# Attention of one batch moved to array quarters and ahead of the last weight loads, in a fused retention and expert kernel

## The chip, the cores and the metric

The kernel runs on one core of one Trainium2 chip. The metric is the device time of one execution in microseconds (us). The kernel before took 515.71 us, the median of 6 runs (515.15 to 519.15).

## What is computed

The reference has two parts, and the output of the first is the input of the second. Cut to what matters:

```python
# q, k, v: 8 batches x 8 heads x 576 positions x 64
scores = (q @ k.T) / 8                       # for each batch and head
Dmat   = gamma[h] ** (i - j) where i >= j, else 0
x      = ((scores * Dmat) @ v), heads side by side   # 4608 tokens x 512

# 4 experts, w1: 512 x 1024, w2: 1024 x 512
p   = probs / (probs.sum(-1) + 1e-9)
out = sum over e of p[:, e] * (relu(x @ w1[e]) @ w2[e])   # 4608 x 512
```

The first part is a retention layer: attention with a decay instead of a softmax. The second sends every token through all four experts, and adds their outputs with weights.

## The kernel before

**Work and order.** The 4608 tokens are cut into nine tiles of 512. A *unit* (nt, e) is tile nt in expert e: an *up* part that makes the hidden values `relu(x @ w1[e])`, and a *down* part that multiplies them with `w2[e]`. There are 36 units, and the order of every instruction is written out by hand: nothing is rescheduled, so each engine works through its own queue in the order in which the Python code issues to it.

**Two ways of working a unit.** The classical way (`up_classical` L522, `downs` L544) takes 32 products of 128 x 128 weights with 512 columns for each part; their lines in the profile are L525 (tile `ph`) and L564 (tile `po`). The other way (`up_fast` L678, class `Down` L625) splits both matrices into 2 x 2 blocks and forms the block product with seven block products instead of eight, 56 products of 256 columns for each part; the lines are L691 (tiles `upP`, `upQ`, `upR`, by PSUM bank) and L645 (`downV`, `downW`). It needs sums of blocks, made by VectorE (DVE): of the weights (`weight_sums` L580, `down_sums` L603), once for each expert; of the tokens (`token_sums` L597), once for each tile; and of the hidden values (`hidden_sum` L608), for each unit. In `up_fast`, DVE reads bank P twice for each half: once into `upR` (L707), once into the hidden values (L715), which GpSimd (POOL) then clamps at zero (L716). TensorE writes that bank again afterwards.

**Attention.** Each batch's 576 positions are four chunks of 128 and a remainder of 64. Three classes work it. `AttP` (L406) is for batch 0: its loads take positions in pairs, its scores and values are products on quarters of the array, 64 rows by 64 columns, and a visit handles four heads by 256 positions. `Att` (L251) is for the others: a visit handles a chunk of 128 positions for all heads, with products on halves of the array. A visit is made of transposes (T), scores (S), the chunk's key-value product (kv), and the output (O), to which the states of the earlier chunks are added through `sbd`. `put_x` (L232) copies the output into the token tiles. The batches from 2 on go through a planner (`Chain`, L779): a list for each engine from which the unit loop takes the next piece at set places, at most when what it needs has been issued.

**The front.** POOL issues the weight loads, which also convert to 16 bits, in its own software DMA queue; SyncE (SP) issues the loads of q, k and v and the plain stores in the hardware queue. Batch 0 is loaded first, then the weights of all four experts one behind the other (L736 to L759), all of them issued by 24 us. SP then loads batch 0's remainder, whose first load waits for the first `w2` (`load_next(w20)`), and after it batch 1 chunk by chunk (`load_piece` L109). On TensorE the front is a list of classical work, `head` (L731, L986): up (0,0), up (0,1), down (0,0), down (0,1), up (0,2), down (0,2), up (0,3), down (0,3), up (1,0). It is cut into groups, counted by `g`, and the dictionary `plan`, filled by `at(g, ...)` (L914 to L984), says what is issued behind which group: batch 0's remainder at 29 to 34, batch 1's four chunks at 39 to 47, and the weight sums in between.

**The loop behind it** (L1019) begins with unit (1,1). Each turn issues `up_fast` of its unit, and between its products the down part of the unit before (`fill`), the planner's pieces and the sums still owed (`pay`). Down (1,0) is the last classical part.

**Outputs.** Tile 0 and the last tile are summed over the experts on the chip (`on_chip` L500) and stored at the end. For the others, expert 0's part is stored by SP, and the others are added in memory by POOL's accumulating stores (L514).

Of the kernel before, what the change touches and what calls it, by code (L numbers as in the profile page):

```python
# [23 lines left out]
def kernel(  # L24
# [66 lines left out]

    def raw_units(b):

        state[b] = {}
        for x in range(4):
            t = wpool.tile([128, 3, H * D], FP32, tag=f"w2s_{x}", name="raw")
            for i, (n, _) in enumerate(SRC):
                state[b][n, x] = t[:, i]

    def load_paired(b):  # L100
        raw_units(b)
        for x, (hf, u) in enumerate(UNITS):
            h = slice(4 * u, 4 * u + 4)
            for n, src in SRC:
                nc.sync.dma_start(
                    out=state[b][n, x].rearrange("p (h x) -> p h x", h=4),
                    in_=src[b, h, 256 * hf:256 * hf + 256, :].rearrange("h (p j) d -> p h (j d)", j=2))
# [48 lines left out]
    load_paired(0)  # L156
# [249 lines left out]
    class AttP(Att):  # L406

        rem_states = (1, 3)

        def cast(self, n, hf, u, eng):  # L410
            if (n, u) == ("k", 0):
                self.half(hf)
            h = slice(4 * u, 4 * u + 4)
            if n != "v":
                self.m[n, hf, u] = att1.tile([128, 2, 4, D], BF16, tag=n + "m", name=n + "m", bufs=3)
            o = self.m[n, hf][:, :, h, :] if n == "v" else self.m[n, hf, u]
            i = self.t[n, 2 * hf + u].rearrange("p (h j d) -> p j h d", h=4, j=2)
            if n in gain:
                g = gain[n][:, NCH + 1 + 2 * hf:NCH + 3 + 2 * hf, h]
                eng.tensor_tensor(o, i, g.unsqueeze(3).to_broadcast([128, 2, 4, D]), op=MULT)  # L420
            else:
                eng.tensor_copy(o, i)
# [71 lines left out]


# [4 lines left out]
    def on_chip(nt):  # L500
        return nt in (0, n_nt - 1)

    def out_pair(nt, e, pair, j):

        if e == 0 or not on_chip(nt):
            acc[nt, j] = apool.tile([128, 2, Dm], FP32, tag="acc", name="acc")
        return acc[nt, j]

    def send(nt, e, pair, j):
        x = slice(nt * NSUB + pair[0], nt * NSUB + pair[1] + 1, pair[1] - pair[0])  # L510
        if e == 0:
# [32 lines left out]
    def downs(nt, e, ring):  # L544

        hT = hTs[nt, e]
        def evacuate(po, ns):
# [3 lines left out]
            if e == 0 or not on_chip(nt):  # L551
                nc.scalar.activation(a, po, Copy, scale=pe)
            else:
                nc.vector.scalar_tensor_tensor(a, po, pe, a, op0=MULT, op1=ADD)
            if not on_chip(nt):
                if ns % 2:
                    send(nt, e, pair, j)
            elif e == E - 1:
                nc.sync.dma_start(out=out[t * 128:(t + 1) * 128, :], in_=a)
# [65 lines left out]
    class Down:  # L625
# [37 lines left out]
        def out(self, i):  # L663
# [5 lines left out]
            if e and on_chip(nt):  # L669
# [5 lines left out]
            if i == 1 and not on_chip(nt):  # L675
                send(nt, e, pair, j)
# [80 lines left out]
    for e in range(2, E):  # L757
        load_w1(e)
        load_w2(e)  # L759
# [4 lines left out]
    for c in range(2):  # L764
        for n in "kqv":
            load_piece(1, n, c)
# [12 lines left out]
    class Chain:  # L779
        def __init__(self):  # L780
# [5 lines left out]
            self.now, self.begun, self.tokens, self.late = 0, {(1, "r"): -1}, 2 * S - R, []  # L786
# [87 lines left out]
        def emit(self, kind, nt, strict=True):  # L874
# [4 lines left out]
            for k, n in need.items():  # L879
# [8 lines left out]
                elif k == "tile":  # L888
                    ok = n <= nt + 2
# [27 lines left out]
    def casts1(*cs):  # L917
        for c in cs:
            for n in "kqv":
                state["a1"].cast(n, c, nc.gpsimd)  # L920

    def begin1():
        state["a1"] = Att(1)
        casts1(0)
        for c in range(2, NCH):
            for n in "kqv":
                load_piece(1, n, c)
        casts1(1, 2)
        load_ahead(7)

# [4 lines left out]

    def rem1_casts():
        for n in "kqv":
            a1().cast_rem(n, nc.gpsimd)
            loads["cast"] += 1
            load_ahead(len(PIECES))  # L940
        a1().dmaT(NCH)

    def a1():
        return state["a1"]
# [3 lines left out]
    at(29, a0.Trem)  # L948
    at(31, a0.Srem, a0.Srem_mask)
    at(34, a0.Orem, lambda: a0.x(NCH, nc.vector))  # L950
    at(25, begin1)
    for c, g in enumerate((39, 41, 43, 45)):
        at(g, lambda c=c: a1().T(c))
        at(g + 1, lambda c=c: (a1().S(c), a1().kv_chain(c)))
        if c > 0:
            at(g + 1, lambda c=c: a1().O(c - 1))
        at(g + 1, lambda c=c: (a1().mask(c, 0), a1().mask(c, 1)))
        if c > 0:
            at(g + 1, lambda c=c: a1().x(c - 1, nc.vector))
    at(47, lambda: (a1().O(3), a1().x(3, nc.vector)))  # L960

    def narrow():
        RINGS["at"] = ("a0", "a1", "a2")
        turn.update(at=0)

    at(42, lambda: casts1(3))
    at(46, rem1_casts)
    at(48, narrow, lambda: state.update(t1=token_sums(1)), lambda: [state["t1"].pop(i)() for i in (0, 0, 1)])

    def sums_at(kind, e, *gs):  # L970
        todo = []
        for i, g in enumerate(gs):
            at(g, lambda i=i: (todo or todo.extend(kind(e)), todo[i]()))
        return todo

    sums_at(weight_sums, 1, 16, 17, 18, 19)
    s0 = sums_at(weight_sums, 0, 20, 21, 22)
    sums_at(weight_sums, 2, 26, 28, 30, 31)
    sums_at(down_sums, 1, 42, 43, 44, 48)
    sums_at(weight_sums, 3, 36, 38, 49, 50)  # L980
    s2 = sums_at(down_sums, 2, 51, 52, 53)
    at(50, lambda: a1().put_krem(nc.gpsimd, a1().qr[:, 1]))
    for g in range(48, 56):
        at(g, lambda: pool(1, 1))  # L984

    head += [up_classical(0, 1), down_groups(0, 0), down_groups(0, 1), up_classical(0, 2), down_groups(0, 2),  # L986
             up_classical(0, 3), down_groups(0, 3), up_classical(1, 0, lead=2, cut=3 * NT // 4)]
    g = 0
    for work in head:
        for _ in work:  # L990
# [3 lines left out]
            if g > 48:  # L994
                chain.now += 1


    turn.update(po=0)
    state["t1"].pop()()
    def stage(nt, e):  # L1000
        return nt * E + e

    begin = {1: (1, 1), 2: (1, 2), 3: (1, 3), 0: (2, 0)}
    owed = [((1, 1), (2, 0), s0[3]), ((1, 1), (1, 3), s2[3])]
    for e in (3, 0):

        use, last = stage(*begin[e]) + 1, stage(*begin[e]) - E + 2
        owed += [(divmod(last if i == 3 else 0, E), divmod(use, E), f) for i, f in enumerate(down_sums(e))]

    def pay(nt, e, late=False):  # L1010
        for x in owed:
            if x[1] <= (nt, e) if late else x[0] <= (nt, e):
# [5 lines left out]
    before, gaps = (1, 0), 0  # L1018
    for nt, e in [(nt, e) for nt in range(1, n_nt) for e in range(E)][1:]:  # L1019
        fast = before >= begin[before[1]]  # L1020
# [8 lines left out]
        def between(i):  # L1029
# [3 lines left out]
            if i == 3:  # L1033
                pool(nt, 4 if gaps < 8 else 3 - g)
# [4 lines left out]
        def fill(i):  # L1039
            if i == 4:  # L1040
                chain.put_late()
            if not fast:
# [29 lines left out]
        def last_sum():  # L1072
            if g == 1 and (nt, e) >= begin[e]:
# [5 lines left out]
        def sums(i):  # L1079


            old, new = before in hsum, (nt, e) >= begin[e]
            turns = {(0, 1): 0 if old else 2, (0, 2): 0 if old else 1, (0, 3): 1,
                     (1, 1): 2, (1, 2): 1, (1, 3): 1}[g, i]
            while (e, g, i) == (0, 0, 2) and front:
# [4 lines left out]
            if g == 1 and new:  # L1090
# [120 lines left out]
```

## Time and profile before

The profile is of one execution. Its span, from the first instruction to the last, is 513.3 us; that execution took 515.11 us on the device, so 1.8 us lie around the span.

| What | Value |
|---|---|
| median of 6 runs | 515.71 us |
| the profiled execution | 515.11 us |
| its span | 513.3 us |
| granted TensorE clock | 0.998 of full |
| TensorE (PE) with a product in it | 504.1 us of the span |
| VectorE (DVE) busy | 374.4 us |
| ScalarE (ACT) busy | 336.0 us |
| GpSimd (POOL) busy | 250.1 us |
| moved by DMA | 76.27 MB, 149 GB/s over the span |

How to read it. "Busy" for PE counts a product from its start to its end, and products overlap in the array; two products of 0.6 us can start 0.44 us apart. So the start-to-start distances in the timeline tell how fast TensorE works, not the durations. In a timeline row the columns are the start in us from the span's start, the length in us, the engine, the line of the kernel, the operation, what it writes and reads, the shape, and the number of instructions that the row merges; what stands in square brackets is the engine's idle time before it and what ended it. In the rows of the DMA queues the columns are the packets, the MB and the share of the 16 DMA engines' time. q0 is POOL's software queue, q1 SP's hardware queue.

### The profile page before, as it was taken

To read this page: it belongs to the slowest core of one execution; us is meant where nothing else is said; L and a number is where in the kernel's file an instruction comes from. 1 tells how busy PE (TensorE), PEld (TensorE's weight loads), DVE (VectorE), ACT (ScalarE), POOL (GpSimd) and SP (SyncE) were. 2 spreads that over 40 slices of the span, in tenths; PEclk is the share of its full clock that TensorE was granted. 3 is DMA by queue.
4 is the path that set the end of the run, shared out by engine and by line. 5 is a ranking of instruction groups with operands and counts; after the bars stand their busy time and mean duration, and the time that the engine had idled before them with its cause. 6 is when DMAs were issued, how large, how long until landed. Compare 5 with 4: busy or idle time off the path is not lost.

```text
span 513.3 us, 12806 instructions
## 1 busy us (share of the span) xinstructions
PE 504.1 (98%) x4934; PEld 405.5 (79%) x4934; DVE 374.4 (73%) x696; ACT 336.0 (65%) x693; POOL 250.1 (49%) x345
## 2 busy tenths in 40 slices
PE   8999999999999999999999999999999999999995
PEld 4644455688888888888888888888888888888885
DVE  5625579888777777768777877886778777667775
ACT  3552264677667766777777776777777767777663
POOL 6802175656734656456645664476457521321012
PEclk9999999999999999999999999999999999999999
DMA  8999998959698799879998999789997652565002
GB/s 236 189 207 201 207 192 201 166 145 187 112 178 192 120 174 160 180 144 185 132 224 138 173 142 219 154 144 153 174 195 121 94 84 84 83 86 81 1 2 82
DMA packets 160749, 76.27 MB, mean 149 GB/s; under 512 B 131724, under 2 KB 144524, under 8 KB 160688
## 3 DMA queue, kind: packets, MB, share of 16 engines
q1 hardware_dynamic: 141648, 44.79, 43.3%
q0 software_dynamic: 18752, 30.41, 39.4%
q8 instruction: 38, 0.62, 0.5%
q10 hardware_dynamic: 288, 0.26, 0.2%
q14 instruction: 23, 0.19, 0.1%
HBM read 45.16 MB, written 31.46 MB: 149 GB/s over the span
## 4 chain that ended last, share of the span: by engine, by line
PE 94%; DVE 4%; DMA 1%; issue 1%; ACT 0%; SPq 0%; DVEq 0%; ACTq 0%
PE upP L691 21%; PE downV L645 20%; PE downW L645 15%; PE upR L691 10%; PE ph L525 7%; PE po L564 7%; PE upQ L691 5%; PE s L328 2%; PE oc L379 1%; PE kvp L346 1%; PE oc L376 1%; DMA raw<-in_q_dram 1%; DVE sT L469 0%; PE warm_out L164 0%; PE last L1131 0%
## 5 line engine op out<-in xcount | busy, mean ns | idle before, releaser
L691 PEld LDWEIGHTS <-wt 128*128 128x128 bf16 x992 | 94.9, 98 | 14.5 <-issue 1.4
L645 PEld LDWEIGHTS <-hT 128*128 128x128 bf16 x960 | 93.7, 98 | 12.0
L716 POOL TENSOR_SCALAR hT<-hT 128x512 bf16<-128x512 bf16 x62 | 38.1, 614 | 108.6 <-DVE hT L715 108.3
L645 PE MATMUL downV<-wt,hT 128*128 128x256 bf16 x480 | 81.8, 272 | 0.0
L691 PEld LDWEIGHTS <-wsum 128*128 128x128 bf16 x744 | 72.6, 98 | 9.1 <-issue 0.2
L707 DVE TENSOR_TENSOR upR<-upP,m 128x512 f32<-128x512 f32 x62 | 43.3, 699 | 48.6 <-ACT downW L651 39.9
L645 PEld LDWEIGHTS <-hsum 128*128 128x128 bf16 x720 | 70.0, 98 | 8.8 <-DVE hsum L617 0.3
L691 PE MATMUL upP<-xT,wt 128*128 128x256 bf16 x496 | 74.4, 272 | 0.7 <-DVE xT L595 0.5
L723 ACT ACTIVATE hT<-upP 128x512 bf16<-128x512 f32 x62 | 37.0, 597 | 52.0 <-PE upP L691 36.8
L514 POOL DMA_DIRECT2D out_dram<-acc x42 | 51.3, 1221 | 30.7 <-ACT acc L672 23.9
L674 DVE TENSOR_SCALAR acc<-downV,probs 128x512 f32<-128x512 f32 x56 | 41.9, 749 | 30.1 <-PE downV L645 29.7
L718 ACT ACTIVATE hT<-upR 128x512 bf16<-128x512 f32 x62 | 37.0, 597 | 31.3 <-PE upR L691 31.3
L709 ACT ACTIVATE hT<-upQ 128x512 bf16<-128x512 f32 x62 | 37.0, 597 | 15.9 <-PE upQ L691 15.9
L715 DVE TENSOR_TENSOR hT<-upP,m 128x512 bf16<-128x512 f32 x62 | 42.7, 689 | 5.7 <-PE upP L691 4.4
L672 ACT ACTIVATE acc<-downW,probs 128x512 f32<-128x512 f32 x56 | 38.6, 689 | 9.1 <-PE downW L645 9.1
L340 POOL TENSOR_SCALAR_AFFINE_SELECT sT<-sT 128x512 bf16<-128x512 bf16 x24 | 15.4, 643 | 57.4 <-ACT sT L339 48.1
L541 ACT ACTIVATE hT<-ph 128x512 bf16<-128x512 f32 x40 | 23.5, 597 | 29.8 <-PE ph L525 29.8
L697 ACT ACTIVATE upQ<-upP 128x512 f32<-128x512 f32 x62 | 37.0, 597 | 2.5 <-PE upP L691 2.3
L691 PE MATMUL upP<-tsum,wt 128*128 128x256 bf16 x248 | 37.3, 273 | 0.0
L691 PE MATMUL upR<-tsum,wsum 128*128 128x256 bf16 x248 | 37.2, 273 | 0.1
L691 PE MATMUL upP<-tsum,wsum 128*128 128x256 bf16 x248 | 37.2, 273 | 0.0
L691 PE MATMUL upQ<-xT,wt 128*128 128x256 bf16 x248 | 37.2, 273 | 0.0
(149 smaller groups left out, 1033.0 us busy)
## 6 DMA issues: line engine op xcount, KB each, us to landing
out_dram<-acc POOLq DMA_DIRECT2D x42, 512.0 KB, 6.4
out_dram<-acc SPq DMA_DIRECT2D x14, 512.0 KB, 4.2
wt<-in_moe_w_dram POOLq DMA_DIRECT2D x6, 1024.0 KB, 25.1
raw_k<-in_k_dram SPq DMA_DIRECT2D x24, 256.0 KB, 4.5
raw_q<-in_q_dram SPq DMA_DIRECT2D x24, 256.0 KB, 4.0
raw_v<-in_v_dram SPq DMA_DIRECT2D x24, 256.0 KB, 4.2
raw<-in_k_dram SPq DMA_DIRECT2D x8, 256.0 KB, 5.5
raw<-in_q_dram SPq DMA_DIRECT2D x8, 256.0 KB, 5.7
```

The costliest lines, as they stand in the source:

```text
L514: i = nc.gpsimd.dma_start(out=out_rows[:, x, :], in_=acc[nt, j], accum_op=ADD)
L645: nc.tensor.matmul(o, lhsT=l[:, k, self.s * 128:(self.s + 1) * 128], rhs=r[:, k], start=(i == 1 and k == 0), stop=(k == NFC // 2 - 1), ski ...
L672: nc.scalar.activation(a, po, Copy, scale=pe)
L674: nc.vector.tensor_scalar_mul(a, po, pe)
L691: nc.tensor.matmul(ps[:, l], lhsT=wa(kc)[:, f:f + 128], rhs=xa(kc), start=(start and l == 0 and kc == 0), stop=(kc == 1), skip_group_check ...
L697: nc.scalar.activation(Q, P, Copy)
L707: nc.vector.tensor_tensor(R_, P, m5, op=ADD)
L709: nc.scalar.activation(hT[:, lo, t0], Q, Relu)
L715: nc.vector.tensor_tensor(h22, P, m5, op=ADD)
L716: nc.gpsimd.tensor_scalar(h22, h22, float("inf"), 0.0, op0=MIN, op1=MAX)
L718: nc.scalar.activation(hT[:, lo, t1], R_, Relu)
L723: nc.scalar.activation(hT[:, hi, t0], P, Relu)
```

## The change

**Batch 1** gets a class `AttQ` on the paired layout. Its four units of four heads by 256 positions run in the order 0, 2, 1, 3. Scores, values and now the key-value products too are products on array quarters. All earlier half-chunk states are added to an output one by one, as nothing is summed up in PSUM any more (`rem_states = (0, 1, 2, 3)` for the remainder as well). The transposes' copies are shared between DVE (k) and ScalarE (q); the token copies go from DVE to ScalarE.

```diff
+    class AttQ(AttP):
+        rem_states = (0, 1, 2, 3)
...
+        def visit(self, new, old):
+            ko = [one_bank(t, [128, 2, C + D], FP32, "ko") for t in ("a2", "o0")]
+            quads = [(a, j, d, c) for a in range(2) for j in range(2) for d in range(2) for c in range(2)]
+            if new:
+                hf, u = new
+                for a, j, d, c in quads:
+                    r, h = slice(64 * c, 64 * c + 64), 2 * a + d
+                    nc.tensor.matmul(ko[c][64 * d:64 * d + 64, a, C:], lhsT=self.m["k", hf, u][r, j, h, :],
+                                     rhs=self.m["v", hf][r, j, 4 * u + h, :], ...)
...
+            if old:
+                self.values(*old, ko)
...
+                    put_x(nc.scalar, slice(2 * u, 2 * u + 2), self.b * S + 256 * hf + c * C, ko[c][:, :, :C])
```

**Loads.** Batch 1 is loaded as four units of three loads on SP, behind batch 0's remainder, and its first load waits for the first half of expert 2's `w1`. Expert 2's `w2` is issued by POOL behind the casts of k and v of the first three units; expert 3's `w1` (two halves) and `w2` behind those of the fourth. Batch 1's remainder follows in SP's queue behind two stores of tile 0. Its casts are issued on POOL in the first gap of unit (1,0).

```diff
-    for e in range(2, E):
-        load_w1(e)
-        load_w2(e)
+    w12 = load_w1(2, 0)
+    load_w1(2, 1)
...
-    for c in range(2):
-        for n in "kqv":
-            load_piece(1, n, c)
+    ORDER1 = (0, 2, 1, 3)
+    for x in ORDER1:
+        load_unit(1, x, w12)
...
+    at(3, lambda: cast1(0, "kv"), lambda: cast1(1, "kv"), lambda: cast1(2, "kv"), lambda: load_w2(2))
+    at(21, a0.Trem)
+    at(22, a0.Srem, a0.Srem_mask, lambda: cast1(0, "q"))
+    at(23, a0.Orem, lambda: a0.x(NCH, nc.scalar))
+    for i, g in enumerate((23, 25, 27, 29)):
+        at(g, lambda i=i: a1.T(*UNITS[ORDER1[i]]))
+        if i < 3:
+            at(g, lambda i=i: cast1(i + 1, "q"))
+        at(g + 1, lambda i=i: visit1(i, i - 1))
+    sums_at(weight_sums, ws, 2, 20, 22, 24)
+    at(24, lambda: cast1(3, "kv"), lambda: load_w1(3, 0), lambda: load_w1(3, 1), lambda: load_w2(3),
+       lambda: load_ahead(6))
```

**Order of the units.** The classical front is shorter: up (0,0), up (0,1), down (0,0), down (0,1), up (0,2). Batch 0's remainder stands behind down (0,1), and batch 1's visits between the eight groups of up (0,2). The loop then begins with (1,0) and (1,1), and (0,3) comes third. Every part from up (1,0) on is in seven products, except down (0,2), which fills unit (1,0). So up and down of (1,0) and of (0,3) change from the classical way to the other.

```diff
-    head += [up_classical(0, 1), down_groups(0, 0), down_groups(0, 1), up_classical(0, 2), down_groups(0, 2),
-             up_classical(0, 3), down_groups(0, 3), up_classical(1, 0, lead=2, cut=3 * NT // 4)]
+    head += [up_classical(0, 1), down_groups(0, 0), down_groups(0, 1), up_classical(0, 2)]
...
+    stages = [(1, 0), (1, 1), (0, 3)] + [(nt, e) for nt in range(1, n_nt) for e in range(E)][2:]
+    order = {s: i for i, s in enumerate([(0, 2)] + stages)}
+    fast_from = order[1, 0]
+    t0, t1 = token_sums(0), token_sums(1)
+    t1.pop(0)()
+    owed = [((1, 0), (1, 1), f) for f in t0]
+    owed += [((1, 0), (0, 3), f) for f in weight_sums(3)]
...
+            if (nt, e, g, i) == (1, 0, 0, 1):
+                visit1(4, 3)
+                t1.pop(0)()
+                front.extend(t1)
...
+            if not old and (g, i) != (0, 1):
+                turns += 3 if (g, i) == (0, 2) else 1 if (g, i) != (1, 1) else 0
```

**Sums.** Those of experts 0 and 1 are made earlier, in the classical front. In unit (1,0) DVE makes, in this order: tile 1's token sums, tile 0's token sums, expert 3's weight sums, and its usual sums of hidden values.

**Outputs.** Tile 0 is summed on the chip for experts 0 and 1 alone; that sum is stored by SP, and experts 2 and 3 are added by POOL's accumulating stores.

```diff
-    def on_chip(nt):
-        return nt in (0, n_nt - 1)
+    def adds(nt, e):
+        return e > 0 and (nt == n_nt - 1 or (nt, e) == (0, 1))
+
+    def sends(nt, e):
+        return nt < n_nt - 1 and (nt, e) != (0, 0)
```

## The prediction, made before the changed kernel ran

> **What bounds the kernel now.** First I read the page's busy lines and the shares of the chain that ended last:
>
> ```profile
> PE 504.1 (98%) x4934; PEld 405.5 (79%) x4934; DVE 374.4 (73%) x696; ACT 336.0 (65%) x693; POOL 250.1 (49%) x345
> ...
> PE 94%; DVE 4%; DMA 1%; issue 1%; ACT 0%; SPq 0%; DVEq 0%; ACTq 0%
> ```
>
> TensorE is the chain. A busy share can hide gaps, so I then read the chain in order of time and TensorE's timeline for the rate of its products:
>
> ```profile
> 34.00 13.81 PE po L564 x64
> 47.82 5.18 PE ph L525 x24
> 89.43 0.60 PE L691 MATMUL upP<-xT,wt 128*128 128x256 bf16 x4
> 89.86 0.60 PE L691 MATMUL upR<-tsum,wsum 128*128 128x256 bf16 x4
> 90.30 1.03 PE L564 MATMUL po<-wt,hT 128*128 128x512 bf16 x4
> ```
>
> In the timeline the first column is a group's start. 64 products 512 columns wide take 13.81 us, 0.216 each; groups of four 256-column products start 0.437 apart, 0.109 each. From 20 us to the tail nearly every start follows at this pace: the waits that the groups show on TensorE after 20 us sum to about 1 us. So the time is the list of products, and a change wins what it strikes off that list and loses every wait it brings. The loads of the front are hidden at present; that is the cover this change spends.
>
> **Units.** A classical unit is 32 wide products, 32 x 0.216 = 6.91 us; one in seven products is 56 narrow ones, 14 groups x 0.437 = 6.12. Both hidden-layer products of (1,0) and (0,3) and both of their output products go over, and the instruction order of the changed kernel confirms it (wide output products 160 to 96, others in step): 4 x 0.79 = **-3.2 us**.
>
> **Batch 1.** Its transposes stay 32. I price the rest from these rows, the first block batch 1 as it is, the second batch 0, which is already in quarters:
>
> ```profile
> 74.03 0.40 PE L328 MATMUL s<-qkT 64*128 64x128 bf16 x8
> 74.36 0.32 PE L346 MATMUL kvp<-vm,km 128*64 128x64 bf16 x8
> 74.51 0.39 PE L376 MATMUL oc<-sT,vm 128*64 128x128 bf16 x8
> 74.83 0.40 PE L379 MATMUL oc<-qkT,sbd 128*128 128x128 bf16 x4
> 75.07 0.38 PE L564 MATMUL po<-wt,hT 128*128 128x512 bf16 x1
> ```
> ```profile
> 19.74 0.42 PE L481 MATMUL o<-sT,vm 64*64 64x128 bf16 x16
> 20.09 0.51 PE L488 MATMUL o<-qkT,sbd 128*128 128x128 bf16 x6
> 20.43 0.82 PE L525 MATMUL ph<-xT,wt 128*128 128x256 bf16 x6
> ```
>
> Start to start, a chunk now costs 0.33 scores, 0.15 key-values, 0.32 values and 0.24 states (three chunks have them), plus 0.1 to enter from a wide product, five times, and 0.1 more for the first key-values: four chunks make 4.5 us. In quarters a set of 16 costs 0.35 where the shape of the products changes behind it. Inside one run of sets I take 0.21 (four abreast, 4 x 0.054, half the 0.109 above); no row shows it alone. For the 16 key-value quarters of 64 columns no row exists: half of two sets of eight at 0.15 is the low end, 0.15, the full two sets 0.30 the high one; I take 0.2. Four visits: scores 3 x 0.21 + 0.35, key-values 4 x 0.2, values 4 x 0.35, 24 state products at 0.058 (1.4), entries 5 x 0.1; the remainder adds 12 products at 0.029 (0.35). Sum 5.4, so **+0.9 us**, bounds +0.3 to +1.6.
>
> Do short products keep that pace? The eight key-value products above start 19 ns apart, the 16 quarter products of 128 columns 22 ns.
>
> [...]
>
> **The loads.** The weights of experts 2 (second half of the pair) and 3 no longer go first; batch 1 does. What that costs depends on how the two DMA queues share. Two stretches of the queue table, 36 to 42 us and 44 to 46 us:
>
> ```profile
> q0 software_dynamic: 614, 1.06, 94.6%
> q1 hardware_dynamic: 612, 0.15, 19.4%
> ```
> ```profile
> q0 software_dynamic: 297, 0.30, 89.5%
> q1 hardware_dynamic: 302, 0.07, 29.5%
> ```
>
> Columns are packets and MB: packet for packet, one each. The weights run at 0.15 MB/us under contention (0.20 alone, 24 to 34 us), a 256-byte load at 0.025 to 0.04. POOL's timeline shows what that did to the remainder's four loads, issued from 31.5 us:
>
> ```profile
> 42.10 1.03 POOL L287 TENSOR_TENSOR krb<-raw_k,gk 64x512 bf16<-64x512 f32 x1 [18.36 <-DMA raw_k<-in_k_dram]
> 46.42 1.03 POOL L287 TENSOR_TENSOR qrb<-raw_q,gq 64x512 bf16<-64x512 f32 x1 [3.29 <-DMA raw_q<-in_q_dram]
> 48.16 0.39 POOL L291 CAST vbd<-raw_v 64x256 bf16<-64x256 f32 x1 [0.70 <-DMA raw_v<-in_v_dram]
> 50.16 0.40 POOL L291 CAST vbd<-raw_v 64x256 bf16<-64x256 f32 x1 [1.60 <-DMA raw_v<-in_v_dram]
> 58.97 1.04 POOL L279 TENSOR_TENSOR km<-raw,gk 128x512 bf16<-128x512 f32 x1 [8.41 <-DMA raw<-in_k_dram]
> ```
>
> Now in order. Five of the eight 1.05 MB weights remain in the first burst: 3.9 MB are written by 34 us, 1.3 remain at 0.15 to 0.20, so it ends near 42. Then SP's queue is alone with batch 1's twelve 256 KB loads. Batch 0's, of the same shape, ran at 2.25 MB in 8 us, 0.93 each: they land from 43.8 to 54. TensorE wants the first pair at 48.7 (the second output unit ends at 47.82, the remainder, now in front, adds 0.9), POOL has cast it by 45, and each later pair keeps 2 us or more: **0** here; without that lead a late load would hold TensorE by as much as it is late.
>
> The third pair's cast (POOL, 51.8) lets POOL issue expert 2's second matrix, behind it expert 3's three pieces; the six casts in front of them are the queue they were moved past. In SP's queue two 512 KB stores of tile 0 follow batch 1, then batch 1's remainder. Two stores and a weight side by side: expert 2's lands at about 63, expert 3's first matrix at 69.4, its second near 75; the remainder at 69.5 (3.4 + 3.4 + 1.7 + 1.7 us behind the stores, which end at 59).
>
> TensorE reaches stage (1,0) at 61.5: eight blocks of 0.86 from 48.7, three transposes more at 0.45, visits of 0.6, 0.9, 1.4 and 0.9. Its waits there:
> - Product three needs tile 1's second sum: last visit ends at +1.5, ScalarE copies until 2.5, the sum 0.42: **0.2 us**, 0 to 0.5.
> - Classical output of (0,2) needs its weights at 63.0: **0**, 0 to 1.5.
> - Four sums of tile 0 stand on DVE between its two reads of that product bank. At the 0.42 each and 0.33 to 0.45 spacing of such sums they fit. With POOL working beside, one ran 1.26 us (xT at 89.78). **0**, up to 1.4.
> - DVE then waits for expert 3's first matrix, 67.9 to 69.4, works four sums (0.7 to 0.9 each), and the addition that TensorE needs at 72.8 is done near 73.5. Two hidden sums and one weight sum follow before the next: **0.8 us** in all, 0 to 3.
> - POOL stands at the remainder's casts from 58, and the first clamp of hidden values queues behind; DVE's hidden sums need that by 72.3. Landing at 69.5 leaves 2 us: **0**, 0 to 6.
>
> As waits, none of these can go below nothing. ScalarE has up to 4.0 us of copies in a visit's cycle of 3.3 to 3.8, by durations; rectifier and copy start 0.5 apart where they last 0.6, and three banks cover it: **0.2 us**, 0 to 1.5. Its token copies come off DVE. Tile 0's four extra accumulating stores cost POOL 4 x 1.22 us off the chain. The stages behind are the same list; batch 2's casts come no earlier than now, and its first scores at (1,1) are the next thing that could be late.
>
> **Sum.** -3.2 + 0.9 + 1.2 = -1.1 us on a profiled execution of 515.1 us (span 513.3 and 1.8 around it): 514.0. The median shown is 515.7, 0.6 above that execution, so the forecast is **514.6**.
>
> **Rivals.**
> (a) The waits don't come, and the attention is at its low end: -3.2 + 0.3, **512.8**. For it: every wait above is under 1 us and behind a load whose time I know to 2 us. Against it: DVE's wait for expert 3 has no spare time.
> (b) Slower: POOL waits on batch 1's remainder. If its loads crawl as now, 18.7 us from issue (31.5) to last cast (50.2), and start only behind the stores at 59, POOL is free at 77.7 and its clamp (0.6) done 6.0 us past 72.3; DVE's in-order queue hands that to TensorE: -2.3 + 6.0 + 1.0, **520.4**. It decides from the time at which the last remainder load lands after 71. For it: expert 3's 2 MB are in the other queue at that time. Against it: 10.6 of those 18.7 us went on the first load, under 2 KB weight packets; here they are 1 KB.
> (c) Batch 1 isn't ready at 48.7, since POOL casts one pair in 1.7 us and the first burst ends later: 2 to 3 us of waits between the blocks, which take the place of the waits above (their DMAs run on meanwhile): -2.3 + 2.5 + 0.4, **516.3**, no change.
>
> **Numbers.** About 0.5%, 2.6 us, is what a measurement here tells from no change, so under 513.1 is faster and over 518.3 slower. Forecast 0.45, (c) 0.12: no change 0.57. (a) 0.25. (b) 0.18, of which I keep the lower half in the range: 512.5 to 519.0.
>
> **What would show it.** Right: 96 wide output products; hidden-layer groups 0.437 apart from about 62 us, with idle TensorE under 2 us between 48 and 80, ended by DVE; visits of 0.9 to 1.4 us. Wrong: idle at the first transposes near 49 (c), POOL idle on the remainder's loads beyond 72 with DVE's hidden sum behind it (b), a wide output product waiting for weights near 63, or visits over 1.5 us without idle, which would put the quarters' price above the bound.

## The result, and the profile after

The changed kernel takes 517.88 us, the median of 18 runs (516.88 to 521.94), and the kernel before 515.79 us in 37 runs (514.37 to 519.15). The ratio is 1.0052, 95% interval 1.0038 to 1.0066. The forecast was 514.6: 1.1 us faster. It became 2.1 us slower.

The profiled execution of the changed kernel took 517.39 us, with a span of 515.7 (before 515.11 and 513.3). From its page, the busy lines and the shares of the chain that ended last:

```profile
PE 502.3 (97%) x5142; PEld 415.2 (81%) x5142; DVE 391.8 (76%) x722; ACT 348.2 (68%) x736; POOL 253.9 (49%) x351
...
PE 87%; DVE 6%; issue 2%; DMA 2%; ACT 1%; SPq 1%; POOL 0%; DVEq 0%; ACTq 0%
```

TensorE's share of the chain fell from 94 to 87%: the end is now set in part by what TensorE waits for. I added up its starts and idle gaps from the first product of down (0,0) to the first product of the last unit's down part, in both traces:

| us | before | after | difference |
|---|---|---|---|
| the whole stretch | 467.85 | 470.92 | **+3.07** |
| four units by price: 128 wide products at 0.216 go, 224 narrow ones at 0.437 for four come | | | -3.18 |
| TensorE's idle gaps in it | 0.82 | 4.08 | +3.26 |
| the rest: attention, entries between shapes, what a gap costs beyond its length | | | +2.99 |

The head is 0.26 us shorter, the tail 0.46, so the span grew by 2.4. The units' row is a price and no measurement of its own: the numbers of products are as forecast, and the pace is the same in both traces. In the terms of the prediction, its sum was -3.2 for the units, +0.9 for batch 1 in quarters and +1.2 for waits; what came was -3.18, +2.99 for all that is neither units nor gaps, and +3.26 of gaps. So two terms were too small, each by about 2.1 us.

The gaps stand in three places. First the visits of batch 1, TensorE's timeline at the first and the last of them:

```profile
49.83 0.32 PE L533 MATMUL ko<-vm,km 64*64 64x64 bf16 x16
51.03 0.58 PE L539 MATMUL s<-qkT 64*64 64x128 bf16 x16 [0.88 <-ACT qkT L522]
...
62.24 0.42 PE L539 MATMUL s<-qkT 64*64 64x128 bf16 x16 [0.42 <-ACT qkT L522]
```

The scores wait for ScalarE's copy of the transposed queries: 0.88, 0.35, 0.01 and 0.42 us in the four visits, 1.66 together. (e4, e6 and e8 leave all this as it is, and there the waits are 1.05, 1.00 and 1.00 in the first visit, 0.20, 1.64 and 0.21 in the second, 0.22, none and none in the last: the first is steady, the others are not.) Why ScalarE is late at the first visit is told by its own timeline and by VectorE's and POOL's at that time:

```profile
50.59 0.66 ACT L522 ACTIVATE qkT<-pt 128x256 bf16<-128x256 bf16 x2 [1.59 <-DVE qkT L520]
```
```profile
47.38 0.68 DVE L433 TENSOR_TENSOR qm<-raw,gq 128x512 bf16<-128x512 f32 x1
47.98 1.53 DVE L667 TENSOR_TENSOR wsum<-wsum,wt 128x1024 bf16<-128x1024 bf16 x1
49.43 0.74 DVE L636 SCALAR_TENSOR_TENSOR acc<-po,probs,acc 128x512 f32<-128x512 f32 x1
50.09 0.41 DVE L520 COPY qkT<-pt 128x512 bf16<-128x512 bf16 x1
```
```profile
47.67 1.29 POOL L433 TENSOR_TENSOR km<-raw,gk 128x512 bf16<-128x512 f32 x1 [0.33 <-DMA raw<-in_k_dram]
```

ScalarE stood 1.59 us until VectorE had copied the keys (L520), for q and k were transposed into one PSUM bank (in e2, with a bank for each, TensorE's wait fell from 0.88 to 0.23 us). VectorE came late since a weight sum took 1.53 us, beside POOL's cast; with POOL idle such a sum took 0.69 (e1, at 78.56). In the last visit nothing of that holds: VectorE copied the keys at 60.75, and ScalarE had three state and token copies and a rectifier in front of its query copies at 61.31.

The second place is batch 2's first scores, the third VectorE, whose addition is late at the third unit:

```profile
85.55 0.40 PE L340 MATMUL s<-qkT 64*128 64x128 bf16 x8 [0.78 <-DMA qkT<-km]
...
97.09 0.60 PE L772 MATMUL upP<-xT,wt 128*128 128x256 bf16 x4 [0.56 <-DVE upR L788]
```

Each such gap costs 0.16 to 0.19 us more than its length, by the start-to-start distance against the group's median.

### The profile page after: what moved, and what is told of

Its sections match the earlier page's. It is cut to its first block, busy times and chain, and to the rows that moved or that the text cites. A ratio compares the mean times of both kernels' runs of the same rounds, so it can differ in the third digit from the quotient of the medians.

```text
span 515.7 us, 13331 instructions
## 1 busy us (share of the span) xinstructions
PE 502.3 (97%) x5142; PEld 415.2 (81%) x5142; DVE 391.8 (76%) x722; ACT 348.2 (68%) x736; POOL 253.9 (49%) x351
## 4 chain that ended last, share of the span: by engine, by line
PE 87%; DVE 6%; issue 2%; DMA 2%; ACT 1%; SPq 1%; POOL 0%; DVEq 0%; ACTq 0%
PE upP L772 21%; PE downV L726 21%; PE downW L726 15%; PE upR L772 11%; PE upQ L772 5%; PE po L645 4%; PE ph L609 3%; PE s L340 2%; PE oc L391 1%; PE kvp L358 1%; DMA raw<-in_q_dram 1%; PE oc L388 1%; DVE hsum L698 1%; DVE sT L482 1%; DVE qm L433 1%
## 5 line engine op out<-in xcount | busy, mean ns | idle before, releaser
L772 PEld LDWEIGHTS <-wt 128*128 128x128 bf16 x1056 | 100.9, 98 | 16.5 <-issue 2.5
L726 PEld LDWEIGHTS <-hT 128*128 128x128 bf16 x1024 | 100.1, 98 | 12.6
L797 POOL TENSOR_SCALAR hT<-hT 128x512 bf16<-128x512 bf16 x66 | 41.1, 623 | 112.5 <-DVE hT L796 112.3
L726 PE MATMUL downV<-wt,hT 128*128 128x256 bf16 x512 | 87.2, 272 | 0.0
L772 PEld LDWEIGHTS <-wsum 128*128 128x128 bf16 x792 | 77.5, 98 | 9.4
L726 PEld LDWEIGHTS <-hsum 128*128 128x128 bf16 x768 | 74.2, 98 | 10.9 <-DVE hsum L698 1.0
L772 PE MATMUL upP<-xT,wt 128*128 128x256 bf16 x528 | 79.2, 272 | 0.8 <-DVE upR L788 0.7
L598 POOL DMA_DIRECT2D out_dram<-acc x46 | 56.2, 1222 | 33.2 <-ACT acc L753 27.4
L783 ACT ACTIVATE m<-upR 128x512 f32<-128x512 f32 x66 | 39.5, 598 | 0.7 <-PE upR L772 0.7
L772 PE MATMUL upR<-xT,wsum 128*128 128x256 bf16 x264 | 39.6, 273 | 0.0
```

Of the source, the lines that this page charges most:

```text
L598: i = nc.gpsimd.dma_start(out=out_rows[:, x, :], in_=acc[nt, j], accum_op=ADD)
L726: nc.tensor.matmul(o, lhsT=l[:, k, self.s * 128:(self.s + 1) * 128], rhs=r[:, k], start=(i == 1 and k == 0), stop=(k == NFC // 2 - 1), ski ...
L772: nc.tensor.matmul(ps[:, l], lhsT=wa(kc)[:, f:f + 128], rhs=xa(kc), start=(start and l == 0 and kc == 0), stop=(kc == 1), skip_group_check ...
L783: nc.scalar.activation(m5, R_, Copy)
L797: nc.gpsimd.tensor_scalar(h22, h22, float("inf"), 0.0, op0=MIN, op1=MAX)
```

## The experiments

All times stand against the kernel before on the same chip, 515.6 to 515.9 us. "To (1,0)" is the time from the first product of down (0,0) to the first product of up (1,0) in the profiled execution; it is 30.2 us in the changed kernel. A trace shows one execution, and not always one near the median: e2's took 516.42 us, e4's 520.37 and e6's 527.05.

| Run | median us | ratio, 95% interval | to (1,0) |
|---|---|---|---|
| the changed kernel | 517.88 | 1.0052, 1.0038 to 1.0066 | 30.2 |
| e1 sums later | 520.64 | 1.0098, 1.0082 to 1.0113 | 28.3 |
| e2 query bank | 519.41 | 1.0057, 1.0035 to 1.0078 | 30.1 |
| e3 tokens on VectorE | 519.11 | 1.0061, 1.0046 to 1.0077 | 31.7 |
| e4 scores later | 518.21 | 1.0052, 1.0033 to 1.0072 | 29.9 |
| e5 e1, w2 of expert 2 earlier | 519.23 | 1.0076, 1.0058 to 1.0095 | 29.0 |
| e6 w2 of expert 3 later | 523.91 | 1.0161, 1.0130 to 1.0193 | 32.5 |
| e7 e5 and e6 | 526.23 | 1.0210, 1.0179 to 1.0241 | 28.3 |
| e8 stores left out | 516.48 | 1.0033, 1.0020 to 1.0046 | 30.5 |
| e9 e1, half of w2 left out | 516.53 | 1.0023, 1.0013 to 1.0032 | 28.4 |
| e10 e9 and e8 | 516.46 | 1.0016, 1.0004 to 1.0028 | 28.3 |
| e11 sums behind the last casts | 519.73 | 1.0075, 1.0057 to 1.0094 | 28.3 |
| e12 e11, both left out | 515.11 | 0.9995, 0.9985 to 1.0006 | 28.3 |

**e1, the weight sums out of the visits.**

```diff
-    sums_at(weight_sums, ws, 2, 20, 22, 24)
...
-    owed += [((1, 0), (1, 2), f) for f in ws[2][3:]]
+    owed += [((1, 0), (1, 2), f) for f in weight_sums(2)]
```

> Expert 2's first three weight sums leave the batch-1 steps and are paid for in stages (1,0) and (0,3). Theory A (the visits' waits in front of the scores come from VectorE, whose weight sum took 1.53 us and whose q casts 1.29 to 1.46 us there, so that the key copy and behind it ScalarE's query copy come late): TensorE's wait in front of the scores of the first visit falls from 0.88 us to below 0.2, of the second from 0.35 to below 0.2; with 0 to 0.4 us of new VectorE waits in (1,0) and (0,3) the kernel takes 516.9 to 517.3 us at before's 515.8. Rival B (ScalarE's own queue sets all four): waits stay at 0.88, 0.35 and 0.42 and the time at 517.9. If the sums are in the way wherever they stand, the 1.0 us comes back as waits on VectorE in the two stages: 517.9 again.

All four visits' waits went, the last as well, though that one is missing in e6 and e8 too (TensorE's timeline of e1; the gap row of the first visit is now without brackets):

```profile
50.03 0.32 PE L533 MATMUL ko<-vm,km 64*64 64x64 bf16 x16
50.23 0.58 PE L539 MATMUL s<-qkT 64*64 64x128 bf16 x16
...
66.25 1.02 PE L645 MATMUL po<-wt,hT 128*128 128x512 bf16 x4 [2.04 <-DMA wt<-in_moe_w_dram]
...
68.61 1.06 PE L772 MATMUL upQ<-xT,wt 128*128 128x256 bf16 x4
```

So theory A holds: VectorE's load made the first visits late. But TensorE came to (1,0) 1.96 us sooner only to stand 2.04 us for expert 2's second matrix, which lands at 66.2 us. Then four narrow products took 1.06 us instead of 0.60. The windows of e1 (columns: TensorE's busy time and weight loads, VectorE, ScalarE, POOL, then the granted clock, the DMA share, GB/s) say why:

```profile
66.00:67.30 1.30, 1.05 (x6) 0.56 (x6) 0.00 (x0) 0.00 (x0) 0.39 (x1) 1.00 1.25 207
67.30:70.70 3.40, 3.18 (x14) 1.93 (x14) 1.75 (x5) 1.19 (x2) 0.40 (x1) 0.50 1.23 199
70.70:74.00 3.30, 3.30 (x23) 2.06 (x22) 2.73 (x5) 1.88 (x3) 0.95 (x1) 1.00 1.23 196
```

For 3.4 us, from 1.1 us behind the wait on, the granted clock was 0.50, which by estimate, as half of the 3.4, costs some 1.7 us more. The moved sums came back as waits of 0.54 and 0.70 us on VectorE near 80 and 85 us. No theory had the matrix or the clock in it; the time is 3.3 us above its expectation.

**e2, a bank of their own for the queries.**

```diff
-            pt = one_bank("o1", [128, 2, 2, 256], BF16, "pt")
+            pt = [one_bank(t, [128, 2, 256], BF16, "pt") for t in ("a0", "o1")]
```

> The query transposes of batch 1 go into a bank of their own (that of the scores), so that ScalarE's query copies no longer wait for VectorE's key copy of the same bank. Theory A with the bank as the coupling: ScalarE copies at once, while the key copy is still bound to VectorE; the first visit's wait falls from 0.88 us by ScalarE's 0.67 us of copies to about 0.2, the second's from 0.35 to 0.1, the third and fourth (0 and 0.42) stay; time 516.9 to 517.2. Rival B (ScalarE's queue alone is late): no wait changes, 517.9. A new wait could come where the transposes now need the scores' bank read by the mask of the visit before: then a wait stands ahead of the transposes of the second to fourth visit.

The first visit's wait fell from 0.88 to 0.23 us and is now for VectorE's key copy, the second's went; and the new wait is there, ahead of the second transposes (TensorE's timeline of e2):

```profile
50.81 0.42 PE L539 MATMUL s<-qkT 64*64 64x128 bf16 x16 [0.23 <-DVE qkT L520]
...
52.88 0.38 PE L517 MATMUL pt<-ident,qm 128*128 128x128 bf16 x4 [0.69 <-DVE sT L551]
```

The shared bank was the coupling, and VectorE the cause. The profiled execution took 516.4 us, 0.5 less than expected, but the median of six was 519.4, and the interval overlaps the changed kernel's; what the other five met, no trace shows.

**e3, the token copies on VectorE.**

```diff
-                    put_x(nc.scalar, slice(2 * u, 2 * u + 2), self.b * S + 256 * hf + c * C, ko[c][:, :, :C])
+                    put_x(nc.vector, slice(2 * u, 2 * u + 2), self.b * S + 256 * hf + c * C, ko[c][:, :, :C])
```

> Batch 1's output columns are copied to the token tile by VectorE instead of ScalarE. Theory A' (the fourth visit's 0.42 us, the waits inside the score sets and the 0.09 and 0.06 at the start of (1,0) come from ScalarE, which has four to six copies ahead of the query copies): these fall to below 0.1 each, a gain of 0.4 to 0.7 us. Against it VectorE, already late at the first two visits, has two copies more per visit from the second on (0.3 to 0.4 us each): the second visit's 0.35 may grow to 0.7. Sum 517.2 to 518.0. Rival (ScalarE is not the limit of the last visits): nothing falls, 517.9 to 518.5.

The last visit's wait fell from 0.42 to 0.09 us, which agrees with ScalarE's copies as its cause but does not show it, as e6 and e8 have no wait there with the copies still on ScalarE. The second visit's grew from 0.35 to 1.52, more than twice what I had expected. VectorE has no room in the visits.

**e4, batch 2's first scores one place later.** In the first half of (1,1) the planner gives TensorE nothing.

```diff
-            if i == 3 or chain.todo["PE"] and "any" in chain.todo["PE"][0][1]:
+            if (nt, e, g) != (1, 1, 0) and (i == 3 or chain.todo["PE"] and "any" in chain.todo["PE"][0][1]):
```

> Batch 2's first score set may not be put into the first half of stage (1,1) and goes in at the next place, behind one more pair of products. Theory B2 (the 0.78 us in front of that set, and 0.17 within it, are the wait for the DMA transpose alone, which lands at 85.5 us, 0.95 us after TensorE is ready): the wait goes, nothing takes its place, 516.9 to 517.1. Rival (the next link of the batch's chain becomes late by as much, since the masks, states and outputs are each put one place later): part or all comes back in (1,1) and (0,3), 517.4 to 518.0.

The rival holds in what the trace shows: 0.47 us were still waited there, and then TensorE waited for VectorE, and VectorE for a store (TensorE's and VectorE's timelines of e4):

```profile
111.83 0.60 PE L726 MATMUL downV<-wt,hT 128*128 128x256 bf16 x4 [1.71 <-DVE acc L755]
```
```profile
111.03 0.75 DVE L755 TENSOR_SCALAR acc<-downV,probs 128x512 f32<-128x512 f32 x1 [2.99 <-DMA out_dram<-acc]
```

There are two output buffers, and the one to be written was still being stored. The same wait stands in e3 (1.38 us) and e11 (2.54), and not in the profiled execution of the changed kernel. It is another place where transfers end last. The median, 518.2, is not to be told from the changed kernel's.

**e5 to e7, the order of the loads.** e5 is e1 with expert 2's second matrix issued one pair of casts sooner. e6 is the changed kernel with expert 3's second matrix issued by POOL behind its first clamp. e7 has both.

```diff
-    at(3, lambda: cast1(0, "kv"), lambda: cast1(1, "kv"), lambda: cast1(2, "kv"), lambda: load_w2(2))
+    at(3, lambda: cast1(0, "kv"), lambda: cast1(1, "kv"), lambda: load_w2(2), lambda: cast1(2, "kv"))
```
```diff
-    at(24, lambda: cast1(3, "kv"), lambda: load_w1(3, 0), lambda: load_w1(3, 1), lambda: load_w2(3),
+    at(24, lambda: cast1(3, "kv"), lambda: load_w1(3, 0), lambda: load_w1(3, 1),
...
+            if gaps == 3:
+                load_w2(3)
```

> Expert 2's weight sums leave the batch-1 steps (as in the run of that edit alone, where the visits' waits fell from 1.65 us to nothing, TensorE reached stage (1,0) 1.6 us sooner, then stood 2.04 us for expert 2's second matrix, landed at 66.2 us, and ran at a granted clock of 0.50 from 68 to 70 us), and that matrix is now issued one pair of casts sooner. Theory (the matrix is the next late thing, and the drop of the clock follows the 2 us wait): it lands near 64.5, the wait is below 0.6 us, the clock stays at 1.00 between 64 and 80, and stage (1,1) starts at 77.5 to 78 instead of 81.2; time 516.5 to 517.3 at before's 515.8. Rival (the transfers share one saturated set of engines, so that what the matrix gains batch 1's last pairs lose): the wait moves to the third or fourth visit, 1 to 2 us, 517.5 to 519.

The matrix landed at 65.7 instead of 66.2, and TensorE reached it 0.7 us later than in e1, since a wait came in the fourth visit. The rival had the place, but its cause is not shown: the last pair was cast by 56.1 us, and what ended the wait is ScalarE's rectifier. What stands beside the matrix was pushed back: batch 1's remainder ended at 73.6 us (66.8 in the changed kernel), expert 3's first matrix at 72.3 (70.8), and batch 2's first scores waited again (TensorE's timeline of e5):

```profile
62.01 0.42 PE L539 MATMUL s<-qkT 64*64 64x128 bf16 x16 [0.82 <-ACT hT L625]
76.30 0.60 PE L772 MATMUL upP<-xT,wt 128*128 128x256 bf16 x4 [0.72 <-DVE upR L788]
79.01 0.60 PE L772 MATMUL upP<-tsum,wt 128*128 128x256 bf16 x4 [0.82 <-DVE hT L796]
...
88.19 0.40 PE L340 MATMUL s<-qkT 64*128 64x128 bf16 x8 [0.92 <-DMA qkT<-km]
```

The first of the two on VectorE is the wait that the prediction had at 0.8 us: VectorE stood 1.76 us for expert 3's first matrix. The second is the moved sums' again. The clock stayed at 1.00, so that part of the theory held.

> Expert 3's second matrix, which landed at 77.35 us and is first read at 83.8, is issued behind the first clamp of stage (1,0), some 14 us later, so that batch 2's first pieces (landed at 77.7 to 82.3, issued at 67.1 to 69.3) have the transfers to themselves from 71 us. Theory (batch 2's first scores wait 0.78 us because its pieces share the transfers with that matrix): the pieces land 2 to 4 us earlier, the first scores do not wait, 516.9 to 517.1. Rival 1 (the casts on GpSimd stand behind its second clamp anyway, which ends at 77.75): the wait stays, 517.9. Rival 2 (the matrix itself is then late for VectorE's sum at 83.8, and VectorE, which works in order, holds the additions TensorE needs): a wait on VectorE of 1 us or more near 85 to 90, 518 to 520.

Batch 2's first two pieces landed at 73.9 and 75.1 instead of 77.7 and 79.0, as expected. It brought nothing: POOL cast them at 81.2, right behind its second clamp, which was rival 1. The transposes were then issued beside the late matrix and a store, and took 6.6 and 7.5 us to land; TensorE stood 4.85 us, and the clock fell to a half twice (timeline and windows of e6):

```profile
56.91 0.58 PE L539 MATMUL s<-qkT 64*64 64x128 bf16 x16 [1.64 <-ACT qkT L522]
93.10 0.61 PE L340 MATMUL s<-qkT 64*128 64x128 bf16 x8 [4.85 <-DMA qkT<-km]
```
```profile
58.00:61.40 3.40, 3.40 (x15) 1.68 (x14) 1.84 (x4) 2.64 (x9) 1.12 (x2) 0.50 1.12 170
...
92.40:99.20 6.80, 6.10 (x36) 4.33 (x37) 2.48 (x4) 2.00 (x5) 0.61 (x1) 0.52 1.19 223
```

The second visit's 1.64 us came with it, though the edit is behind that point. VectorE's timeline has the cause: a weight sum that lasted 0.68 us in the changed kernel lasted 2.12, from 53.99 on, beside two of POOL's casts (54.49 to 56.58), and the key copy came behind it at 56.03:

```profile
53.99 2.12 DVE L668 TENSOR_TENSOR wsum<-wt,wsum 128x1024 bf16<-128x1024 bf16 x1
```

> The three moves together: expert 2's weight sums in stages (1,0) and (0,3), its second matrix one pair of casts sooner, expert 3's second matrix behind the first clamp. If the late links are the ones named (visits 1.65 us, batch 2's first scores 0.95 us) and nothing else takes their place: 517.9 less 2.6, 515.3, no change against before's 515.8. If VectorE's load in the two stages comes back as waits (0.54 and 0.70 us in the run with the sums moved): 516.0 to 516.8. If the transfers are only shuffled: 517.5 or more.

e7 met the same: 6.69 us at batch 2's first scores, 526.2 us. In these three, moving loads only moved the wait.

**e8 to e10, transfers left out.** In e8 tile 0's stores of expert 2 are gone (expert 3's then follow the plain ones). In e9, besides e1's edit, half of expert 2's second matrix is set to zero instead of loaded. e10 has both.

```diff
     def sends(nt, e):
-        return nt < n_nt - 1 and (nt, e) != (0, 0)
+        return nt < n_nt - 1 and (nt, e) not in ((0, 0), (0, 2))
```
```diff
+        nc.gpsimd.memset(w2_sb[e][:, NFC // 2:], 0.0)
...
+        return nc.gpsimd.dma_start(out=w2_sb[e][:, :n], in_=moe_w2[e].rearrange("(fc p) d -> p fc d", p=128)[:, :n])
```

> Tile 0's two stores of expert 2's share (512 KB each, accumulating) are left out, so the output lacks that share for tile 0; all else is as in the changed kernel. They are in flight from 73.1 to 82.4 and from 84.4 to 92.8 us. Theory (the stores that tile 0 now makes for expert 2 and 3, priced by me at POOL's issue time alone, take transfer time that batch 2's pieces and transposes need): the transposes, which took 4.7 us from issue to landing, take 2 to 3, the first scores' wait of 0.78 us falls below 0.2, POOL's queue is 2.5 us shorter, 516.5 to 517.0. Rival (the wait is set by the pieces' own landing at 77.7 and 79.0 us and the casts behind them, ahead of the stores): the wait stays at 0.6 or more, 517.5 to 517.9.

Without the stores the two transposes take 2.5 us each from issue to landing (4.7 and 2.5 with them), and the scores' wait falls from 0.78 to 0.24 us. What ends that wait is the second transpose, of the keys: it takes 2.5 us in both, but is issued sooner behind a first one that takes less, and counted from the first product of (1,0) it lands 0.56 us earlier (21.15 instead of 21.71). From the answers on the transposed tile, e8 and then the changed kernel:

```profile
L309 SPq DMA_TRANSPOSE qkT<-qm x1: 1195/1195/1195, 81.4 to 81.4; - x1
...
DMA to landing us min/median/max: 2.5/2.5/2.5
```
```profile
L309 SPq DMA_TRANSPOSE qkT<-qm x1: 2638/2638/2638, 80.3 to 80.3; - x1
...
DMA to landing us min/median/max: 2.5/3.6/4.7
```

The time is at the lower end of its expectation, the wait a little above it. The interval overlaps the changed kernel's, so it is the landing and the wait, more than the time, that show the effect. The prediction had charged these stores to POOL's issue alone.

> Expert 2's weight sums in stages (1,0) and (0,3), and only the first half of expert 2's second matrix is loaded, the other half being set to zero in the front, so the output lacks half of that expert's inner dimension. Theory (behind the visits' waits stands the landing of that matrix, and nothing on an engine): it lands near 61 to 63 us, TensorE does not wait for it, the clock stays at 1.00, stage (1,0) starts near 62.2 and (1,1) 14.6 later at 76.8, against 78.4 in the changed kernel and 81.2 with the sums moved alone; expert 3's weights and batch 2's pieces land 2 us earlier too; 516.0 to 516.8 with what VectorE's sums cost there. Rival (VectorE's added sums hold the two stages whatever the transfers do): (1,1) at 78 or later, 517.5 or more.

The matrix landed at 62.4; no wait over 0.1 us in the visits, none for it, the mean clock of the execution 0.998 (3.4 us at half would take 0.003), batch 2's first scores without a wait. The two waits on VectorE from the moved sums stayed, 0.53 and 0.47 us, so that (1,1) came 15.3 us behind (1,0), where 14.6 had been expected, at 78.4; that much the rival had right. The time is 516.5 us, as expected, and not the rival's.

> The two edits before together: weight sums moved, half of expert 2's second matrix, none of tile 0's stores of expert 2. If the change's cost is its waits and these come from transfers that it packs in front of 90 us, what is left is the four units less the dense price of the quarters and VectorE's waits: 515.8 - 3.2 + 1.2 + 1.3 = 515.1, range 514.5 to 515.8. If the quarters or the units were mispriced, no leaving out of transfers brings it below 516.5.

Missed: 516.5 instead of 515.1. By the profiled execution (515.56) it would have been inside. The waits of 0.54 and 0.69 us on VectorE are nearly all of TensorE's gaps from the visits to 100 us, which left two readings: the moved sums, or POOL's work beside VectorE. And 516.5 is the bound that had been set for mispriced quarters: they were, as the next section shows.

**e11 and e12, the sums in a third place.**

```diff
-    sums_at(weight_sums, ws, 2, 20, 22, 24)
+    sums_at(weight_sums, ws, 2, 28, 30, 31)
```

> Expert 2's first three weight sums stay in the front, but behind the last query cast (steps 28, 30, 31 instead of 20, 22, 24). Theory (the visits' waits come from VectorE's load in the first two visits; behind them stands the landing of expert 2's second matrix at 65 to 66 us): the first two visits' waits go as they did with the sums in the stages, TensorE reaches stage (1,0) 1 to 1.5 us sooner and then stands 1 to 2 us for the matrix; if the clock halves behind that, 519 to 520, if not, 517.4 to 518. No gain either way. Rival (the visits are the end of it): 516.3 to 516.8.

Again the visits lost their waits, and the matrix took them over, with half the clock behind it (timeline and windows of e11):

```profile
66.68 1.86 PE L645 MATMUL po<-wt,hT 128*128 128x512 bf16 x4 [2.73 <-DMA wt<-in_moe_w_dram]
```
```profile
66.30:69.70 3.40, 3.02 (x11) 1.51 (x11) 0.00 (x0) 0.27 (x1) 0.65 (x2) 0.50 1.23 204
```

> The same places for the sums, with half of expert 2's second matrix and tile 0's stores of expert 2 left out. Theory (in the run with both left out the 0.54 and 0.69 us on VectorE in (1,0) and (0,3) came from the sums moved there): these two waits go, at most 0.4 us comes for tile 1's second sum at the head of (1,0); 0.8 to 1.2 us less than that run's 516.5, so 515.3 to 515.7, at or just below before's 515.8. Rival (they come from GpSimd's clamp and casts slowing VectorE, wherever the sums are): waits of 0.5 us stay, 516.3 or more.

With the transfers out of the way and the sums in this place, both waits on VectorE are gone, and the time is 515.11, a little below its expectation. So the 0.5 us waits were the moved sums. The stretch from the first down product to the last unit takes 467.35 us here, 0.50 less than before, with 1.05 us of gaps. (Seven wide products are missing from this trace, and the 0.47 us of idle time that they leave are not counted. The profiled execution of e12 took 518.78 us, for the clock was at a half from 16.6 to 26.9 us, ahead of that stretch.)

## Why the prediction was wrong, step by step

- **Units, -3.2.** Right, as far as it can be told apart: -3.18 at the pace of the traces.
- **Batch 1 in quarters, +0.9 (0.3 to 1.6).** This step failed: too low, above all in the score sets. The prediction's own sign of it was a visit over 1.5 us without idle time, and the third visit is one, 1.63 us from 57.61 to 59.24 (TensorE's timeline of the changed kernel):

```profile
57.61 0.32 PE L533 MATMUL ko<-vm,km 64*64 64x64 bf16 x16
57.94 0.58 PE L539 MATMUL s<-qkT 64*64 64x128 bf16 x16
58.32 0.42 PE L565 MATMUL ko<-sT,vm 64*64 64x128 bf16 x16
58.67 0.73 PE L571 MATMUL ko<-qkT,sbd 128*128 128x128 bf16 x10
59.24 1.03 PE L609 MATMUL ph<-xT,wt 128*128 128x512 bf16 x4
```

  Start to start that is 0.33 for the key-values, 0.38 scores, 0.35 values and 0.57 states, where the prices were 0.2, 0.21, 0.35 and 0.58. Values and states held here; 0.21 is the price of which the prediction said "no row shows it alone", and for the key-values it had no row either. In e10, whose visits have no wait over 0.01 us, the four visits' own products take 5.59 us from start to start, without idle time: key-values 0.93 (said 0.80), scores 1.66 (0.98), values 1.62 (1.40, the last set alone takes 0.56), states 1.38 (1.40). Before they took 4.02, as priced. With the remainder's twelve products more (+0.19, not 0.35) this is +1.76, beyond the upper bound. All that is neither units nor gaps is +2.59 in e10, +2.45 in e12 and +2.99 in the changed kernel; what these have above +1.76, 0.7 to 1.2 us, lies mostly in the experts' products beside changes of shape and behind gaps, and is not parted further. The 16 key-value products take 0.15 to 0.32 us, 9 to 20 ns each (0.20 in the first visit of e1, from 50.03 to 50.23).
- **ScalarE's copies, 0.2 (0 to 1.5).** This step failed. The visits waited 1.66 us. I had added up ScalarE's durations in a cycle and left out that its query copy comes behind VectorE's key copy of the same bank, for which it stood 1.59 us, and that a sum of VectorE can last over twice as long beside POOL's casts (1.53 us against 0.69), though I had a row for that (1.26 us against 0.42) and used it for stage (1,0) alone. e1 and e2 show the parts.
- **Batch 2's first scores, "the next thing that could be late", at 0.** Failed: 0.78 us of wait, 0.95 with what follows it. I had placed its casts and not its transfers; e8 shows what the stores of tile 0 take from them.
- **DVE's wait for expert 3's first matrix, 0.8.** Not there: the matrix landed at 67.7 and 70.8, VectorE stood 0.21 us for it, TensorE not at all. VectorE was late further on instead, +0.7 us of gaps against before, the largest at 97 us (0.56), where two hidden sums took 0.91 and 1.15 us beside POOL's casts (their medians in that trace are 0.42 and 0.43).
- **Classical output of (0,2), weights at 63.0, 0 (0 to 1.5).** No wait, but not for the reason given: they landed at 64.9, and TensorE was 2.3 us later than I had said. Without the visits' waits it is 2.0 to 2.7 us and half a clock (e1, e11). Two errors covered each other.
- **The other landings** were near: expert 3's second matrix at 77.4 (said 75), the remainder at 66.8 (69.5), batch 1 from 44.8 to about 54.6 (43.8 to 54). Rivals (b) and (c) did not come: POOL's first clamp was done at 71.9, and there was no gap at the first transposes.
- **The slower rival** needed one late load. What came was many waits of under 1 us, from two causes: VectorE packed beside POOL's casts, and transfers that are all needed earlier than before. The first covers the second: e1 and e11 take the first away and the second appears.

So even with its late transfers left out (e12), the change only ties with the kernel before: the +2.45 takes most of what the units give. No order of the same transfers that I ran beats it. Why 4 of the 18 runs of the changed kernel lie at 520.7 to 521.9 us is open. They are 2.8 to 4.1 us above the median, more than a store's buffer (1.4 to 2.5 in e3, e4, e11) or one stretch at half the clock (1.7) costs alone, and neither was seen in the one trace of that kernel. By estimate, 1.7 of 518 us, such a stretch takes 0.003 off an execution's mean clock; two of the four have 0.998, so it was not that in them.

## What to carry to other kernels

When work moves to where the transfers are already dense (a DMA share of 1.1 to 1.25 in most of the windows above), price each wait by what is late behind it, not by its own length: taking away 1.7 us of waits here cost 2.8 us more. Price a product from a row of its own kind: the two prices here that no row showed came out too low, one of them by nearly half. Add up an engine's work in a short stretch with the durations it has beside its neighbours (a weight sum here 1.53 us beside a cast, 0.69 with POOL idle), and look for the buffer that ties two engines together. And count an added store as transfer time for whatever lands in the same microseconds (a transpose here 4.7 us with the stores, 2.5 without), not only as time to issue.

## What the runs showed of the hardware

- **Waits and the clock.** With waits of 1.64 (e6), 2.04 (e1) and 2.73 us (e11) the granted clock fell to 0.50 for 3.4 us, and with 4.85 (e6) and 6.69 us (e7) for 6.8; by estimate half of a drop of 3.4 us is lost, 1.7. In the head, where TensorE had no product in 1.40 us from 8 to 11 (e4) and in 0.81 us from 15 to 17 (e12), it fell for 3.4 us from 11.3 on in e4 and for 10.2 from 16.6 on in e12. With 1.52 (e3), 1.71 (e4) and 2.54 us (e11, from 109.5 us) it did not fall. So the length of a wait alone does not decide. The drops last one, two and three times 3.41 us. Counted from the drops in steps of that length, which is an estimate, e11's 2.54 us is cut by a step's end into 1.14 and 1.40, while e1's 2.04 and e6's 1.64 lie in one step each. No run varied where a wait lies, so what decides is not shown.
- **VectorE beside POOL.** A weight sum of 128 x 1024 in 16 bits took 0.69 us with POOL idle (e1, at 77.84 and 78.56), 1.53 beside POOL's cast (the changed kernel, at 47.98) and 2.12 beside two (e6); a hidden sum took 0.42, the median of 66, and 1.15 beside POOL's cast (the changed kernel, at 94.48). The additions of the two reads of bank P, with an operand in PSUM, stayed at 0.68 to 0.70, all 132 in the changed kernel. Why the one kind slowed and the other did not is not shown.
- **A DMA transpose** of 128 x 512 took 2.5 us from issue to landing without tile 0's stores of expert 2 (e8), 4.7 beside a 512 KB accumulating store (the changed kernel), and up to 7.5 beside such a store and a weight load (e6).
